# Four raw weight buffers in attention, PSUM pools kept open for six blocks of M, and another set-up ahead of the first scores

## The chip, the cores and the metric

One core of one Trainium2 chip. The metric is the device time of one execution in microseconds. Three runs of the kernel before are shown, and one execution with the hardware profiler, from which all rows below come.

## The reference

Causal attention with a bias from cumulative sums, then two layers on its 2304 x 512 output, all in float32; the weights come as float64 numbers.

```python
cum  = cumsum(max(s, 0), axis=-1)                      # q, k, v: 4 batches, 8 heads, 576 x 64
scores = where(causal, -1e9, q @ k.T / 8 + min(-(cum_i - cum_j), 0))
attn = softmax(scores) @ v                             # x: 2304 x 512
y = ((x @ w1) * (x @ w2) @ w3) @ w_out                 # w1, w2: 512 x 1024, w3: 1024 x 1024, w_out: 1024 x 512
h = y @ w_in                                           # 512 x 1024
solu = h * softmax(h)
out = layernorm(solu) * g_ln @ w_out2                  # 1024 x 512
```

## The kernel before, in words

Every product of the layers is made from float32 numbers split in a high and a low f32r word, three matmuls for each (high x high, high x low, low x high). The work is staged as follows.

**Attention** runs over 32 heads in the steps loop (L555). Per head: the scores (`sc`, L170 and L178/L179), row maxima on DVE (L192, into `STAT`), the exponential on ACT (L196), sums and reciprocals (`normalise`, L225 to L233), transposes on PE (`tr`, L265 to L281) and the product with V (`av`, L298). POOL makes the low words of the scores' operands (L100, `QK`).

**The first layer** runs under attention in `ab_unit` (L326): a = x w1, copied to SBUF by ACT (`a_sb`, L338), b = x w2, and DVE's product g = a b out of PSUM (`g_sb`, L346), which goes to DRAM. The last batch's units have no attention beside them; they fill PE from about 325 to 393 us.

**Weights** come as raw pairs of 32-bit words, 512 KB to a load (L407, the `stage` tiles), and are made into float32 by one ACT instruction (L363) and three of DVE (L369, L370, L374), then into a high word (ACT, L95) and a low word (DVE, L100). A list of jobs sets their order. `load_jobs` issues loads as long as fewer than `stg[1]` are out, and `pump(n)` converts n of them; the table PUMP says how many are converted in which step. In attention `stg` is two buffers of the pool `at`; for M it is set to four buffers of another pool.

**M** = w3 w_out is one matrix for two layers. `m_unit(f)` (L632 to L642) makes one of its eight blocks: 24 matmuls of 128x512 (L637) into one PSUM tile, then `MH` on ACT and `ML` on DVE (L100). The words of w3 are two tiles `w3h` and `w3l` per block half, converted in M's stage, with other weights (`IT..`, `IB..`) among them. The loop over f stands at L909 and following.

**The second layer and the rest**: x = g M in `x2_half` (L721; `gh` and `gl` are the words of g, read back from DRAM), then h (L753), the softmax and layer norm, turned tiles (L817) and the output (L847).

PSUM tiles come from two pools at a time, `PSP`. During attention's last part they are `psE` (two banks) and `psF` (six). These are closed at L662, ahead of M, and `psC` and `psD` (four each) are opened in their place.

The order of instructions on each engine is not the program's own: a scheduler with a simulated timeline sets it, and `tc.issue_after` pins an instruction behind another. So an edit in one place can move instructions in others.

**The start** (L481 to L533): eight dummy products of zeros (`zp`, L485) on PE; s loaded into one half of `s_zero`, whose other half POOL sets to zero as the scan's second operand; POOL's memsets of the operands' extra rows (`aug_rows`: two blocks of zeros, a pair of rows of ones and one of -1 for each of two heads); on DVE the scaling (L504) and the scan (L505); then the loads of the sums (`load_aug`, L148 and L149), DVE's memsets for the third head (L512 to L514), POOL's diagonal mask (L521, L522) and its constants for `STAT`, `PT` and `VT` (L527 to L532).

Of the kernel before, what the change touches and what calls it, by code (L numbers as in the profile page):

```python
# [8 lines left out]
F32 = mybir.dt.float32  # L9
# [3 lines left out]
AF = mybir.ActivationFunctionType  # L13
ALU = mybir.AluOpType
AX = mybir.AxisListType
PSUM = bass.MemoryType.PSUM
# [10 lines left out]
def tile_attention_moe(  # L27
# [15 lines left out]
    nc = tc.nc  # L43
    B, H, D, _, S = qkT.shape
    NH = B * H
# [6 lines left out]
    HS = S // 2  # L52
# [4 lines left out]
    for i in range(4, 0, -1):  # L57
# [7 lines left out]
    ps_ctx = ExitStack()  # L65
    PSP = [
        ps_ctx.enter_context(tc.tile_pool(name="psA", bufs=2, space=PSUM)),
        ps_ctx.enter_context(tc.tile_pool(name="psB", bufs=4, space=PSUM)),
    ]
# [38 lines left out]
    wmask = at.tile([128, S], F32, name="wmask")  # L108
# [284 lines left out]
    jobs = []  # L393
    loaded = []

    stg = [at, 2]

    def stage(src):
        raw = stg[0].tile([128, CW, 2], U32, tag="stage", bufs=stg[1], name="stage")
# [83 lines left out]
    zp = smalltile("zp")  # L483
    for i in range(8):
        nc.tensor.matmul(zp[:, 0:HS], zz[:, 0:128], zz, start=True, stop=True)  # L485
    s_zero = at.tile([NH, 2, S], F32, tag="qk2", bufs=2, name="s_zero")
    s_sb, zero = s_zero[:, 0], s_zero[:, 1]
    nc.sync.dma_start(out=s_sb, in_=s.rearrange("b h t -> (b h) t"))
    load_head(0)
    if NQ >= 1:  # L490
        load_head(1)
    cum = at.tile([NH, 2, S], F32, tag="qk2", bufs=2, name="cum")[:, 0]
    CK = at.tile([NH, 2, S], F32R, tag="P", bufs=PB, name="CK")
    nc.gpsimd.memset(zero, 0.0)

    def aug_rows(q_, k_):
        nc.gpsimd.memset(q_[0:64].bitcast(F32), 0.0)
        nc.gpsimd.memset(k_[0:64].bitcast(F32), 0.0)
        nc.gpsimd.memset(q_[0:2].bitcast(F32), 1.0)
        nc.gpsimd.memset(k_[32:34].bitcast(F32), -1.0)  # L500

    for i in range(2):
        aug_rows(QN[i], KN[i])
    nc.vector.tensor_scalar(out=s_sb, in0=s_sb, scalar1=0.0, scalar2=1.0 / SCALE, op0=ALU.max, op1=ALU.mult)  # L504
    nc.vector.tensor_tensor_scan(out=cum, data0=s_sb, data1=zero, initial=0.0, op0=ALU.add, op1=ALU.add)  # L505
    for i in range(2):
        load_aug(i, cum[i:i + 1])

# [1 line left out]
    QN.append(qk3[:, 0])  # L510
    KN.append(qk3[:, 1])
    nc.vector.memset(qk3[0:64], 0.0)  # L512
    nc.vector.memset(qk3[0:2, 0], 1.0)
    nc.vector.memset(qk3[32:34, 1], -1.0)  # L514
    load_head(2)
    load_aug(2, cum[2:3])
    nc.sync.dma_start(out=cumf_scr, in_=cum)
    hi(CK[:, 0], cum, nc.vector)
    lo(CK[:, 1], cum, CK[:, 0])
    nc.sync.dma_start(out=cum_scr.bitcast(F32), in_=CK.bitcast(F32))  # L520
    nc.gpsimd.memset(wmask, 0.0)  # L521
    nc.gpsimd.affine_select(  # L522
        out=wmask[:, S - 128:S], in_=wmask[:, S - 128:S], pattern=[[-1, 128]],
        compare_op=ALU.is_ge, fill=NEG / SCALE, base=0, channel_multiplier=1,
    )
    for st in STAT:
        nc.gpsimd.memset(st, 1.0)  # L527
    for t in PT:
# [1 line left out]
            nc.gpsimd.memset(t[64:128, KO[j]:KO[j] + 64], 0.0)  # L530
    for t in VT:
        nc.gpsimd.memset(t[64:128, 4], 0.0)  # L532
    nc.sync.dma_start(out=gln, in_=g_ln.rearrange("(k p) -> p k", p=128))  # L533

    for f in range(KF):
# [96 lines left out]
    def m_unit(f):  # L632
        ps = smalltile("m")
        for k in range(KF):
            H3, L3 = m_st[f, k // 4]
            for w_, o_ in ((H3, WOH), (H3, WOL), (L3, WOH)):
                nc.tensor.matmul(  # L637
                    ps, w_[:, k % 4], o_[:, k],
                    start=(k == 0 and w_ is H3 and o_ is WOH), stop=(k == KF - 1 and w_ is L3),
                )  # L640
        hi(MH[:, f], ps)
        lo(ML[:, f], ps, MH[:, f])  # L642
# [8 lines left out]
    for i in range(8):  # L651
# [7 lines left out]
            nm[0] += 1  # L659
    behind.clear()  # L660
    right0.close()
    ps_ctx.close()  # L662
    PSP[:] = [
        ctx.enter_context(tc.tile_pool(name="psC", bufs=1, space=PSUM)),
        ctx.enter_context(tc.tile_pool(name="psD", bufs=4, space=PSUM)),
    ]
    HD = DF // 2

    r2 = ctx.enter_context(tc.tile_pool(name="r2", bufs=1, side="right"))
# [239 lines left out]
        wf_load(i)  # L909
    load_g(1)  # L910
    for f in range(nm[0], KF):
        m_unit(f)
        pump(AM[f])
        if f < 6:
            wf_words(f)
        if f == 5:
            split_g(0)
# [101 lines left out]
```

## Time and profile before

| | us |
|---|---|
| median of 3 runs | 738.95 (737.88 to 739.62) |
| the profiled execution's own time | 737.73 |
| its span | 736.0 |
| mean granted clock of TensorE | 0.997 |
| PE busy in the span | 716.7 |
| DVE busy | 504.9 |
| ACT busy | 468.0 |
| POOL busy | 99.5 |

The times of the rows count from the span's start; the profiled execution's time is 1.7 us more than its span. A row of a timeline shows when an instruction began, how long it took, its engine, line and tiles, and in brackets how long the engine had been idle just before it and whose end let it go. PE's matmuls are pipelined, so one can begin before the one ahead of it has ended.

### The profile page before, as it was taken

Reading aid. Unit: us, or ns where it says so; the run is one execution under the profiler, and the core shown is the slowest. Engines: PE = TensorE matmul, PEld = TensorE weight load, DVE = VectorE, ACT = ScalarE, POOL = GpSimd, SP = SyncE. Lnnn points to the kernel's source line nnn. Section 1 sums busy time; section 2 is a strip of 40 time slices with the busy share of each in tenths; the row PEclk is TensorE's granted clock in tenths of the full one; section 3 lists DMA queues with packets and bytes.
Section 4 is the critical chain, followed back from the end, with each engine's and each line's share of the span. In section 5 each row is a group of like instructions: output and inputs, shape, how many; then the busy total and the mean of one; then the engine's idle time right before and its main releaser. Section 6 shows DMA issues by size and latency. Waiting matters only on the chain.

```text
span 736.0 us, 13040 instructions
## 1 busy us (share of the span) xinstructions
PE 716.7 (97%) x4682; PEld 625.0 (85%) x4682; DVE 504.9 (69%) x1267; ACT 468.0 (64%) x985; POOL 99.5 (14%) x102
## 2 busy tenths in 40 slices
PE   9889998999999999999998999999999999999997
PEld 6567978888888899899997889988888988888886
DVE  7987978897678888632887876576747365563651
ACT  4987777898766777732544745577646465564652
POOL 5033313142221331000000000001000000000000
PEclk9999999999999999999999999999999999999999
DMA  4644554655476665614566943253234142304221
GB/s 109 186 126 99 174 161 142 194 144 130 127 221 186 182 188 149 208 61 147 170 215 202 355 149 101 58 110 75 79 82 101 44 123 75 89 12 75 44 57 44
DMA packets 79829, 95.52 MB, mean 130 GB/s; under 512 B 41418, under 2 KB 52682, under 8 KB 79764
## 3 DMA queue, kind: packets, MB, share of 16 engines
q1 hardware_dynamic: 79764, 94.69, 45.0%
q8 instruction: 37, 0.61, 0.3%
q14 instruction: 28, 0.23, 0.1%
HBM read 59.04 MB, written 20.14 MB: 108 GB/s over the span
## 4 chain that ended last, share of the span: by engine, by line
PE 73%; DVE 11%; DMA 8%; ACT 5%; issue 2%; POOL 1%; SPq 0%; ACTq 0%; DVEq 0%; POOLq 0%
PE x L721 14%; PE o L847 13%; PE b L326 10%; PE a L326 10%; PE hX L753 5%; DMA stage<-in_w_dram 5%; PE av L298 4%; PE hZ L753 3%; PE tr L265 3%; ACT P L196 2%; PE sc L170 2%; PE sc L178 2%; DVE P L192 2%; DVE stage L374 2%; PE hW L753 2%
## 5 line engine op out<-in xcount | busy, mean ns | idle before, releaser
L196 ACT ACTIVATE P<-P,STAT 128x576 f32<-128x576 f32 (+4 forms) x160 | 88.3, 554 | 31.5 <-DVE STAT L192 30.9
L100 POOL TENSOR_TENSOR QK<-qk,QK 64x1152 fp32r<-64x1152 f32 x24 | 67.1, 2798 | 167.2 <-ACT QK L95 158.9
L721 PE MATMUL x<-gl,MH 128*128 128x256 f32 x288 | 80.4, 280 | 0.0
L721 PE MATMUL x<-gh,ML 128*128 128x256 f32 x288 | 80.2, 279 | 0.0
L721 PE MATMUL x<-gh,MH 128*128 128x256 f32 x288 | 79.9, 280 | 0.0
L192 DVE CUSTOM_DVE_ANT_0 P<-sc,wmask 128x576 f32<-128x576 f32 (+4 forms) x160 | 70.6, 478 | 4.5 <-PE sc L170 3.2
L326 PE MATMUL a<-xT0h,W 128*128 128x288 f32 x256 | 58.1, 300 | 1.9 <-ACT a_sb L338 1.9
L326 PE MATMUL b<-xT0h,W 128*128 128x288 f32 x256 | 57.6, 299 | 1.5 <-DVE STAT L192 0.8
L847 PE MATMUL o<-OH,lh 128*128 128x512 f32 x144 | 57.1, 397 | 0.2 <-DVE ll L100 0.2
L326 PE MATMUL a<-xT1h,W 128*128 128x288 f32 x256 | 57.2, 298 | 0.0
L847 PE MATMUL o<-OH,ll 128*128 128x512 f32 x144 | 57.0, 396 | 0.0
L847 PE MATMUL o<-OL,lh 128*128 128x512 f32 x144 | 57.0, 396 | 0.0
L326 PE MATMUL b<-xT1h,W 128*128 128x288 f32 x256 | 56.5, 295 | 0.0
L721 PEld LDWEIGHTS x<-gl,MH 128*128 128x128 f32 x288 | 54.2, 188 | 1.3
L817 DVE COPY lt<-turned 128x2048 uint16<-128x2048 uint16 x16 | 21.9, 1368 | 48.4 <-DMA turned<-half 48.4
L721 PEld LDWEIGHTS x<-gh,MH 128*128 128x128 f32 x288 | 54.0, 188 | 1.1
L721 PEld LDWEIGHTS x<-gh,ML 128*128 128x128 f32 x288 | 54.1, 188 | 0.9
L346 DVE TENSOR_TENSOR g_sb<-b,a_sb 128x288 f32<-128x288 f32 x64 | 28.8, 449 | 32.8 <-PE b L326 16.7
L363 ACT ACTIVATE stage<-stage 128x512 f32<-128x512 f32 x56 | 36.9, 674 | 21.2 <-DMA stage<-in_w_dram 18.0
L298 PE MATMUL av<-PT,VT 128*64 128x64 f32 (+4 forms) x384 | 50.1, 395 | 0.0
L231 ACT ACTIVATE P<-P,STAT 128x576 f32<-128x576 f32 x64 | 42.7, 717 | 10.4 <-DVE STAT L226 10.4
L338 ACT ACTIVATE a_sb<-a 128x288 f32<-128x288 f32 x64 | 25.6, 401 | 33.3 <-PE a L326 33.1
(193 smaller groups left out, 1965.5 us busy)
## 6 DMA issues: line engine op xcount, KB each, us to landing
stage<-in_w_dram SPq DMA_DIRECT2D x32, 512.0 KB
g_scr<-g_sb SPq DMA_DIRECT2D x32, 288.0 KB
stage<-in_wo_dram SPq DMA_DIRECT2D x16, 512.0 KB
qk<-in_qk_dram SPq DMA_DIRECT2D x24, 288.0 KB
QK<-QK SPq DMA_DIRECT2D x24, 288.0 KB
gl<-g_scr SPq DMA_DIRECT2D x24, 256.0 KB
wf<-wf_scr SPq DMA_DIRECT2D x22, 256.0 KB
out_dram<-o SPq DMA_DIRECT2D x18, 256.0 KB
```

The lines of the kernel that those rows point to most:

```text
L100: eng.tensor_tensor(out=dst, in0=src, in1=hi_.bitcast(F32), op=ALU.subtract)
L192: mx = nc.vector.tensor_tensor_reduce(out=dst2, in0=ps_in, in1=msk, scale=-SCALE, scalar=BIG, op0=ALU.add, op1=ALU.min, accum_out=st[0:row ...
L196: ex = nc.scalar.activation(out=dst, in_=dst, func=AF.Exp, bias=st[0:rows, ti:ti + 1], scale=-1.0, accum_out=st[0:rows, 5 + ti:6 + ti],)
L231: nc.scalar.activation(out=dst, in_=dst, func=AF.Copy, scale=r)
L298: nc.tensor.matmul(st["ps"][64 * e:64 * e + 64, 448 + c0:448 + c1], vr[:, j, e], PT[(2 * p + e) % 4][:, o + c0:o + c1], **kw,)
L326: nc.tensor.matmul(ps, w_[:, c, fs], x_[:, c, sl], start=(c == 0 and w_ is WH and x_ is XH), stop=(c == KC - 1 and w_ is WL),)
L338: ab_last[0] = nc.scalar.activation(out=a_sb, in_=ps, func=AF.Copy).ins
L346: ab_last[1] = nc.vector.tensor_tensor(out=g[:, sl], in0=ps, in1=st["a"], op=ALU.mult).ins
L363: nc.scalar.activation(out=high.bitcast(F32), in_=high.bitcast(F32), func=AF.Copy, scale=2.0 ** -112)
L721: last = nc.tensor.matmul(ps[:, a], w_[:, k, m * 128:m * 128 + 128], g_[:, k % 2], start=(k == 0 and w_ is MH and g_ is GH), stop=(k == KF ...
L753: last_h[0] = nc.tensor.matmul(ps, x_[:, k], w_[:, k], start=first and k == 0 and x_ is XH and w_ is WH, stop=k == 1 and x_ is XL, skip_gr ...
L847: nc.tensor.matmul(ps, l_[:, k], w_[:, k], start=(k == 0 and l_ is LH and w_ is OH), stop=(k == KF - 1 and l_ is LL),)
```

## The change

In attention the staged weight loads get four raw buffers where there were two. The closing of `psE` and `psF` moves from ahead of M into the loop over M's blocks, ahead of block 6, so that blocks 0 to 5 use tiles of the old pools. At the start, the scan's second operand is the mask tile, which POOL has set to zero; POOL zeroes the first head's operands and DVE the second's; the rows of ones and of -1 are made by six ACT instructions out of `zz`; and POOL's constants for `STAT`, `PT` and `VT` are pinned behind the diagonal mask, which has to wait for the scan.

```diff
-    stg = [at, 2]
+    stg = [at, 4]
...
-    s_zero = at.tile([NH, 2, S], F32, tag="qk2", bufs=2, name="s_zero")
-    s_sb, zero = s_zero[:, 0], s_zero[:, 1]
+    s_sb = at.tile([NH, 2, S], F32, tag="qk2", bufs=2, name="s_sb")[:, 0]
...
-    nc.gpsimd.memset(zero, 0.0)
+    nc.gpsimd.memset(wmask, 0.0)
...
+    def const_rows(q_, k_):
+        for dst, src, value in ((q_[0:2], zz[0:2], 1.0), (k_[32:34], zz[32:34], -1.0)):
+            nc.scalar.activation(
+                out=dst.rearrange("p (a s) -> p a s", a=2), in_=src[:, None, :].broadcast_to((2, 2, HS)),
+                func=AF.Copy, scale=0.0, bias=value,
+            )
+
-    for i in range(2):
-        aug_rows(QN[i], KN[i])
+    for i, eng in enumerate((nc.gpsimd, nc.vector)):
+        eng.memset(QN[i][0:64], 0.0)
+        eng.memset(KN[i][0:64], 0.0)
+        const_rows(QN[i], KN[i])
-    nc.vector.tensor_tensor_scan(out=cum, data0=s_sb, data1=zero, initial=0.0, op0=ALU.add, op1=ALU.add)
+    nc.vector.tensor_tensor_scan(out=cum, data0=s_sb, data1=wmask[0:NH], initial=0.0, op0=ALU.add, op1=ALU.add)
...
-    nc.vector.memset(qk3[0:2, 0], 1.0)
-    nc.vector.memset(qk3[32:34, 1], -1.0)
+    const_rows(QN[2], KN[2])
...
-    nc.gpsimd.memset(wmask, 0.0)
-    nc.gpsimd.affine_select(
+    diagonal = nc.gpsimd.affine_select(
...
+    behind_scan = tc.issue_after(diagonal.ins)
+    behind_scan.__enter__()
     for st in STAT:
         nc.gpsimd.memset(st, 1.0)
...
+    behind_scan.__exit__(None, None, None)
...
-    ps_ctx.close()
-    PSP[:] = [
-        ctx.enter_context(tc.tile_pool(name="psC", bufs=1, space=PSUM)),
-        ctx.enter_context(tc.tile_pool(name="psD", bufs=4, space=PSUM)),
-    ]
...
     for f in range(nm[0], KF):
+        if f == 6:
+            ps_ctx.close()
+            PSP[:] = [
+                ctx.enter_context(tc.tile_pool(name="psC", bufs=1, space=PSUM)),
+                ctx.enter_context(tc.tile_pool(name="psD", bufs=4, space=PSUM)),
+            ]
         m_unit(f)
```

What this does to the order of the instructions is shown at three places. The words in brackets are the semaphores that an instruction waits on, by the engine or the DMA queue that raises them.

PE at the seventh block of M (block 6). Before, blocks run into each other; the rows here are the end of block 6, its first word pair's successor, and the second-layer matmuls that the scheduler put among blocks 6 and 7:

```order
L637 MATMUL m<-WOL,w3h 128x512
L637 MATMUL m<-WOH,w3l 128x512
L637 MATMUL m<-WOH,w3h 128x512 [waits Activation_49]
L637 MATMUL m<-WOL,w3h 128x512
L637 MATMUL m<-WOH,w3h 128x512 [waits Activation_49]
L637 MATMUL m<-WOL,w3h 128x512
L721 MATMUL x_5286<-gh_5214,MH 128x256 [waits DMAHW4_49,DMAHW3_49,DMAHW5_49,DMAHW2_49,DMAHW6_49,DMAHW1_49,DMAHW7_49,DMAHW0_49,DVE_49]
L721 MATMUL x_5286<-gl_4910,MH 128x256
```

And with the change, from the end of block 5 to the beginning of block 6:

```order
L646 MATMUL m<-WOH,w3h 128x512
L646 MATMUL m<-WOL,w3h 128x512
L646 MATMUL m<-WOH,w3l 128x512
L646 MATMUL m<-WOH,w3h 128x512 [waits DVE_49]
L646 MATMUL m<-WOL,w3h 128x512
```

The first matmul of block 6 now has a wait on DVE; before, 20 matmuls of the second layer stood in one row behind L721's first, now three stand there.

DVE at the same place with the change (`ML` is the low word of a block of M, `IT..` low words of other weights, L369 to L374 conversions):

```order
L374 SCALAR_TENSOR_TENSOR stage<-stage 128x512 [waits DVE_49]
L100 TENSOR_TENSOR IT3l<-wf,IT3h 128x512 [waits DMAHW7_49,Activation_49]
L370 SCALAR_TENSOR_TENSOR stage<-stage 128x512 [waits DVE_49]
L100 TENSOR_TENSOR ML<-m,MH 128x512 [waits Activation_49]
L100 TENSOR_TENSOR w3l<-stage,w3h 128x512 [waits PE_49,Activation_49] x2
L374 SCALAR_TENSOR_TENSOR stage<-stage 128x512 [waits DVE_49]
```

This `ML` is block 5's. The order of the kernel before has it at the same place, behind the same conversions but one.

DVE in attention, between the maxima of two heads (`P,STAT_117` and `P,STAT_116`), before:

```order
L192 ISA P,STAT_117<-sc,wmask 128x576 [waits PE_49]
L192 ISA STAT_117 128x1
L374 SCALAR_TENSOR_TENSOR stage<-stage 128x512 [waits DVE_49]
L192 ISA P,STAT_116<-sc,wmask 128x448 [waits PE_49]
L192 ISA STAT_116 128x1
```

With the change:

```order
L192 ISA P,STAT_117<-sc,wmask 128x576 [waits PE_49]
L192 ISA STAT_117 128x1
L369 TENSOR_SCALAR stage<-stage 128x512 [waits DMAHW5_49]
L369 TENSOR_SCALAR stage<-stage 128x512 [waits DMAHW6_49]
L374 SCALAR_TENSOR_TENSOR stage<-stage 128x512 [waits DVE_49]
L100 TENSOR_TENSOR W_124<-stage,W_123 128x4x128 [waits Activation_49]
L192 ISA P,STAT_116<-sc,wmask 128x448 [waits DVE_49,PE_49]
L192 ISA STAT_116 128x1
```

Three instructions of conversion more stand ahead of the second head's 128x448 maxima.

## Rows read from the trace of the kernel before

**Rows 1.** The page's first part: busy time, share of the span, instructions.

```profile
PE 716.7 (97%) x4682; PEld 625.0 (85%) x4682; DVE 504.9 (69%) x1267; ACT 468.0 (64%) x985; POOL 99.5 (14%) x102
```

**Rows 2.** Windows: length; busy PE, PEld, DVE, ACT, POOL (instructions); clock, DMA share, GB/s.

```profile
78.00:104.00 26.00, 23.69 (x178) 21.93 (x177) 25.35 (x76) 22.95 (x63) 8.88 (x3) 1.00 0.51 142
...
104.00:160.00 56.00, 53.03 (x409) 46.35 (x408) 47.27 (x136) 44.87 (x110) 14.40 (x5) 1.00 0.56 168
...
22.00:23.00 1.00, 0.56 (x3) 0.19 (x2) 1.00 (x4) 1.00 (x4) 0.00 (x0) 1.00 1.04 321
```

**Rows 3.** Timeline of PE in attention: start, length, instruction, idle before and its releaser.

```profile
102.11 0.40 PE L326 MATMUL b<-xT0h,W 128*128 128x288 f32 x1 [0.56 <-DVE STAT L192]
...
123.76 0.37 PE L178 MATMUL sc<-QK 128*128 128x288 f32 x1 [1.60 <-issue]
...
158.74 0.40 PE L326 MATMUL b<-xT0h,W 128*128 128x288 f32 x1 [0.28 <-DVE STAT L192]
...
310.96 0.40 PE L326 MATMUL a<-xT0h,W 128*128 128x288 f32 x1 [1.20 <-ACT a_sb L338]
```

**Rows 4.** DVE's waits in 60 to 160 and in 280 to 320: total, times, longest.

```profile
DVE stage L369 <- DMA stage<-in_w_dram: 10.0, 8, 3.1
...
DVE stage L369 <- DMA stage<-in_wo_dram: 5.7, 3, 2.8
```

**Rows 5.** Timeline of ACT around 310 us.

```profile
309.93 0.68 ACT L363 ACTIVATE stage<-stage 128x512 f32<-128x512 f32 x1 [1.33 <-DMA stage<-in_wo_dram]
```

**Rows 6.** Timeline of all engines at the start.

```profile
1.24 7.19 PE L485 MATMUL zp<-zz 128*128 128x288 f32 x16 [1.24 <-DVE zz L482]
...
2.66 2.00 DVE L504 TENSOR_SCALAR s_zero<-s_zero 32x576 f32<-32x576 f32 x1 [1.47 <-DMA s_zero<-in_s_dram]
...
8.66 6.32 PE L170 MATMUL sc<-QKN 128*128 128x288 f32 x24 [0.23 <-DMA QKN<-cum]
```

**Rows 7.** Timeline of PE from the last first-layer matmuls to block 6 of M.

```profile
393.24 0.29 PE L326 MATMUL b<-xT1l,W 128*128 128x288 f32 x1
393.38 0.29 PE L326 MATMUL b<-xT1h,W 128*128 128x288 f32 x1
395.72 0.50 PE L637 MATMUL m<-WOH,w3h 128*128 128x512 f32 x1 [2.05 <-DVE g_sb L346]
...
398.19 0.63 PE L637 MATMUL m<-WOL,w3h 128*128 128x512 f32 x1
398.62 0.63 PE L637 MATMUL m<-WOH,w3l 128*128 128x512 f32 x1
...
430.11 0.39 PE L637 MATMUL m<-WOH,w3h 128*128 128x512 f32 x1
```

**Rows 8.** The chain that ended last, at the end of M: start, length, piece.

```profile
439.20 5.00 PE m L637 x22
444.20 8.99 PE x L721 x77
```

**Rows 9.** Windows, one us of M behind the wait (columns as in rows 2).

```profile
397.00:398.00 1.00, 1.00 (x4) 0.81 (x3) 0.77 (x2) 0.71 (x1) 0.00 (x0) 0.50 0.47 180
```

**Rows 10.** Timeline of DVE in M.

```profile
415.32 0.43 DVE L369 TENSOR_SCALAR stage<-stage 128x512 uint32<-128x512 uint32 x1 [2.20 <-DMA stage<-in_w_dram]
...
433.43 0.69 DVE L100 TENSOR_TENSOR ML<-m,MH 128x512 fp32r<-128x512 f32 x1
```

**Rows 11.** Timeline of DVE: low words of staged weights in attention.

```profile
84.02 1.96 DVE L100 TENSOR_TENSOR W<-stage,W 128x512 fp32r<-128x512 f32 x1
...
86.59 2.46 DVE L100 TENSOR_TENSOR W<-stage,W 128x512 fp32r<-128x512 f32 x1
...
99.59 1.79 DVE L100 TENSOR_TENSOR W<-stage,W 128x512 fp32r<-128x512 f32 x1
...
102.97 0.65 DVE L100 TENSOR_TENSOR W<-stage,W 128x512 fp32r<-128x512 f32 x1
```

**Rows 12.** Timeline of POOL in the same stretch.

```profile
82.74 5.76 POOL L100 TENSOR_TENSOR QK<-qk,QK 64x1152 fp32r<-64x1152 f32 x2 [13.42 <-ACT QK L95]
```

## The prediction, before the changed kernel was run

> **What bounds the kernel now.** I read the page's busy shares first: PE is busy for 716.7 of 736.0 us, DVE for 504.9, ACT for 468.0 [rows 1]. So there are only some 19 us that any edit of waits can win, and the next question is where they lie. The timeline of PE answers it, by the idle that it prints behind an instruction: apart from the start and the tail there are idle spots up to 160 us, one at 311 us and one ahead of M at 395.72 us [rows 3, 7]. The table by windows gives their sums: PE is busy for 23.69 of the 26.00 us from 78 to 104, so 2.31 are idle, and for 53.03 of the 56.00 from 104 to 160, so 2.97 [rows 2]. Elsewhere between 160 and 393 us, and from 444 us on, PE has no idle that matters: a delay or a gain in M reaches the end one for one, because everything behind it is PE's own work (the chain of waits is a chain of PE rows there [rows 8]).
>
> The two groups of idle spots are not alike. In 78 to 104 us DVE itself is busy for 25.35 of 26.00 [rows 2]: PE waits there for an engine without slack, as in the spot at 102.11 us, which ends with the row statistics of L192 [rows 3]. In 104 to 160 us, and ahead of 311 us, the wait on a staged load comes first: the table of DVE's waits puts 10.0 us in 8 waits on the load that L369 reads, up to 3.1 us each, in the stretch 60 to 160, and 5.7 us in 3 waits in 280 to 320 [rows 4]. On ACT the same shows as 1.33 us ahead of the L363 at 309.93, which takes 0.68 [rows 5]; the `a_sb` copy of L338 is queued behind it, and PE's 1.20 us at 310.96 end with that copy [rows 3].
>
> **The change part by part.**
>
> *Four raw buffers.* Loads go out one or two places earlier on SP, four together at the first. A conversion that waits for its load no longer holds DVE and ACT. I count as gone the four spots between 123.76 and 158.74 us (all 2.97 us of that window) and the 1.20 at 310.96 [rows 2, 3]. A spot costs a little more than its idle: matmuls follow each other at 393.38 - 393.24 = 0.14 us (0.13 over several), while one alone takes 0.29 [rows 7], so each restart loses another 0.16. Sum: 2.97 + 1.20 + 5 x 0.16 = 4.97 us won. Lower bound: only the two that are longest go, 1.60 + 1.20 + 2 x 0.16 = 3.1. I take the upper end, since DVE's 10.0 us of waiting is over three times the idle that it gave to PE.
>
> On SP two loads of attention rows (L161) now stand behind a staged load. A staged load is 512 KB, at 321 GB/s [rows 2] 1.63 us. I take nothing for it, since no spot of [rows 3] ends with a load of attention rows; with that cover gone it is 2 x 1.63 = 3.3 us.
>
> The 2.31 us in 78 to 104 I leave as they are: no load ends them. There the same edit moves work the wrong way: the order shows three conversions more (two L369, one low word of L100) ahead of the 128x448 maxima of one head, and six to eight by the next head. Bounds are zero and 2.31 + 4 x 0.16 = 2.95 gained, and 3.4 lost (first rival); zero is nearest to what the rows show, since the number of conversions is the same and only their place changes.
>
> *The start.* ACT's rows of ones and the shorter POOL queue can bring the first scores forward only to where the eight dummy products end: those occupy PE from 1.24 for 7.19, so to 8.43, and the first score matmul is at 8.66 with 0.23 idle [rows 6]. So 0.23 is the ceiling, and I take it. DVE's two new memsets lie in its 1.47 us of idle ahead of L504 [rows 6], and DVE loses two memsets later. POOL's held constants come after the scan, ahead of the time of first use. If that cover were gone, the loss would be that of seven memsets of some 0.5 us.
>
> *PSUM pools.* This part has two effects of opposite sign. First, M's first product no longer waits for the last `g_sb` on DVE; it waits for ACT alone, which is done. PE's 2.05 us ahead of 395.72 go, and M starts at 393.38 + 0.13 = 393.51 [rows 7]. With them goes the clock: after that idle the granted clock is 0.50 from 397 to 398 us, the level of 1.2 GHz [rows 9], matmuls follow at 398.62 - 398.19 = 0.43 us instead of 5.00 / 22 = 0.227 [rows 7, 8], and over eight of them that is 8 x 0.20 = 1.6 us.
>
> Second, the wait comes back ahead of block 6. Its first matmul opens the new pools, and by the order it waits for DVE: for the last eviction out of the old pools, the `ML` of block 5. That `ML` stands on DVE behind a queue with no idle. Before, DVE comes out of a wait for a load at 415.32, then works without a break; its `ML` of block 5 is at 433.43, 18.1 us and 32 instructions later [rows 10]. The order leaves all but one of them (31), and the load that opens the run is one of M's, whose buffers are not part of the change. So that `ML` starts at 433.43 - 0.57 = 432.86 and ends with its 0.69 at 433.55. PE is there long before: 144 matmuls of six blocks at 0.227 from 393.51 end at 426.2. **PE idles for 7.3 us**, then starts block 6 at 433.57, where before it began it at 430.11 [rows 7]. The 21 second-layer matmuls that filled PE among blocks 6 and 7 before are not there to help; three are left, by the order.
>
> From there: 48 matmuls x 0.227 = 10.91, three of L725 at 8.99 / 77 = 0.117 = 0.35 [rows 8], and the clock lost again after the idle: nothing at best, 1.6 as behind the 2.05 us of idle above, or 2.9 as in the cold start, where 16 passes took 7.19 / 16 = 0.449 and the 24 behind them 6.32 / 24 = 0.263 (16 x 0.186 = 2.9) [rows 6]. The idle is longer than the one that cost 1.6 and the array is not as cold as at the start, so 2.2. M ends at 433.57 + 10.91 + 0.35 + 2.2 = 447.03. To stand where before stood at 444.20 - 0.17 = 444.03 (all of M and 21 of L721 done [rows 8]) 18 more second-layer matmuls are needed: 18 x 0.117 = 2.10, so 449.13. **M costs 5.1 us**, between 2.9 and 5.8 by the clock's bounds.
>
> **Sum**: -0.23 - 4.97 + 5.1 = -0.1 us. The profiled execution took 737.73, 1.2 below the median of the three runs shown, 738.95; the sum taken from either leaves it where it was. I predict 738.9 against the median. With the bounds of the gaps and of the clock the forecast's own range is 736.5 to 741.5. A measurement of this kernel can tell about 0.2%, 1.5 us, from no change.
>
> **The rivals.**
>
> *Conversions in the way (slower).* In 78 to 104 us DVE has 0.65 us to spare [rows 2]. Six conversions more ahead of the maxima, at the 18.1 / 32 = 0.57 us at which DVE takes one in M [rows 10], are 3.4 us, all of it on the path of the softmax that PE waits for: 738.9 + 3.4 = 742.3. It decides once more than the 1.5 us that a run can tell, two or three conversions, reach PE. There is a second way to nearly the same price. A low word `W` takes 0.65 us alone, at 102.97, but 2.46 at 86.59 [rows 11], while POOL's L100 has 5.76 us of work from 82.74 on [rows 12]: 1.81 us more. Three such words are held so before the change, from 84.02 to 99.59 [rows 11], and two more would give 3.6. The Trainium skill's page "SBUF — State Buffer", section "Who interferes with whom", states a rule for this: a DVE instruction with two inputs in SBUF and a GpSimd instruction that reads SBUF exclude each other, and the one that comes second waits for the whole of the other. The trace agrees, with the 0.65 and the 2.46. For it: no slack there, and the order shows the words moved. Against it: a conversion that is done early is missing later, and one of the words may now come ahead of POOL's start at 82.74.
>
> *The DVE-bound spots go too (faster).* Once loads are never awaited, the same work starts earlier, and DVE may enter 78 us with less left to do. All of 2.31 + 4 x 0.16 = 2.95 us goes: 736.0. Against it: those spots wait for DVE, which stays busy.
>
> *Block 6 does not wait.* If the new pools take over bank by bank, or `ML` of block 5 is done early, the change does more than I read in it: M is then bound by its `w3` words on DVE, whose last come where they came before, so M costs about nothing and 738.9 - 5.1 = 733.8 is left. Against it: one wait on DVE stands in the order at that matmul, and DVE's queue ahead of it is full.
>
> **How the numbers follow.** Forecast 0.50, of which 0.34 within 0.2%, 0.09 faster (the clock costs nothing after the idle) and 0.07 slower (it costs as in the cold start and the small spots stay). Conversions in the way 0.25, slower. DVE-bound spots gone 0.20, faster. Block 6 without wait 0.05, faster. So faster 0.34, same 0.34, slower 0.32. The range from 735.4 to 742.6 takes in the first rival's price and the second's, and leaves out the last and the ends where two mishaps add up.
>
> **What would show it.** Right: the table of DVE's waits without L369's 10.0 and 5.7 us; no PE idle at 124 and 311 us; first scores at about 8.4 us; M's first product without a wait; then some 7 us of idle ahead of the first L646 of block 6, ended by DVE, and a granted clock near 0.5 for some us behind it. Wrong: block 6 starting within 2 us of the end of block 5, a longer sum of PE idle in 78 to 104 us, or low words of over 1.5 us in larger number than three.

## The result, and the profile after

The changed kernel takes 746.39 us (median of 6 runs, 744.73 to 748.31) against 738.82 before: a ratio of 1.0107 [1.0089, 1.0126], 7.6 us slower. The forecast was 738.9. The profiled execution took 744.73 with a span of 742.9 and a mean granted clock of 0.991; the other five had 0.984 to 0.986.

The page's busy shares, to hold against [rows 1]:

```profile
PE 718.5 (97%) x4682; PEld 627.4 (84%) x4682; DVE 506.8 (68%) x1267; ACT 471.5 (63%) x991; POOL 94.2 (13%) x95
```

PE is busy for nearly as long; the span has 6.9 us more, 5.1 of them idle on PE. The clock is a part of both: span times what the mean granted clock lacks to 1 is 736.0 x 0.003 = 2.2 us before and 742.9 x 0.009 = 6.7 us after. This is an estimate of what the clock took, and an upper one: in M of the changed kernel the clock lacks 3.41 us from 390 to 460 us, a part of it while PE idles, and costs 2.4 (worked out below). Four points that both traces have show where they came in: the first score matmul, the last matmul of the first layer, the start of M's last matmul with 21 matmuls of the second layer behind PE (the changed kernel has done 3 of them by its last `m`, at 448.55, so 18 x 0.117 are added), and the last matmul. The third is called the end of M from here on.

| | before | after | difference |
|---|---|---|---|
| first scores | 8.66 | 7.78 | -0.88 |
| last first-layer matmul | 393.38 | 396.55 | +3.17 |
| end of M | 443.81 | 450.66 | +6.85 |
| last matmul | 731.85 | 738.81 | +6.96 |

So in these two executions attention lost 4.05 us behind the start's 0.88, M 3.68, and the rest 0.11.

**Attention.** DVE's waits in 60 to 160 us, the longest first, to hold against [rows 4]:

```profile
DVE PT L97 <- PE tr L265: 3.8, 1, 3.8
DVE stage L370 <- ACT stage L363: 2.8, 2, 1.9
DVE STAT L225 <- ACT P L196: 2.5, 2, 1.7
```

The 10.0 us on staged loads are gone from the top of the table, as are the 5.7 us around 300 us. But PE's idle spots (stretches in which PE has no matmul) have not gone. They are fewer and longer; the timeline of PE, to hold against [rows 3]:

```profile
79.44 0.47 PE L178 MATMUL sc<-QK 128*128 128x448 f32 x1 [0.93 <-DVE g_sb L346]
...
91.90 0.61 PE L326 MATMUL b<-xT0h,W 128*128 128x288 f32 x1 [2.67 <-DVE g_sb L346]
...
106.37 0.40 PE L326 MATMUL b<-xT0h,W 128*128 128x288 f32 x1 [2.15 <-DVE STAT L192]
...
131.26 0.37 PE L326 MATMUL b<-xT0h,W 128*128 128x288 f32 x1 [2.81 <-DVE g_sb L346]
```

All end with DVE. From 60 to 165 us the trace of before has 8 spots with 5.19 us in sum, none over 1.7; this one has 4 with 8.56. And behind two of them the clock is at its lower level; windows (columns as in rows 2):

```profile
78.00:104.00 26.00, 22.40 (x156) 20.58 (x155) 25.01 (x65) 21.08 (x50) 8.39 (x3) 0.93 0.53 154
104.00:160.00 56.00, 50.97 (x384) 44.63 (x383) 45.98 (x131) 42.84 (x108) 13.67 (x5) 0.97 0.53 153
...
93.00:94.00 1.00, 1.00 (x6) 1.00 (x6) 1.00 (x7) 0.78 (x3) 0.00 (x0) 0.50 0.92 288
```

Summed over windows of one us from 60 to 165, what the granted clock lacks to 1 is 3.42 us, where before it was 0.00. The spot at 311 us is gone, worth 1.20. Together: -0.88 for the start, +3.37 of idle, +3.42 of clock, -1.20, and -0.80 for five restarts less at 0.16 is +3.9; 3.17 were measured, and 0.7 stay unexplained. The 0.00 of before is one execution's; the table behind experiment 15 has others with the same order of instructions that lost as much clock as the changed kernel.

What DVE does in front of the spots, in its timeline:

```profile
83.92 2.70 DVE L370 SCALAR_TENSOR_TENSOR stage<-stage 128x512 uint32<-128x512 uint32 x1
...
87.23 2.44 DVE L370 SCALAR_TENSOR_TENSOR stage<-stage 128x512 uint32<-128x512 uint32 x1
...
101.48 2.55 DVE L374 SCALAR_TENSOR_TENSOR stage<-stage 128x512 uint32<-128x512 uint32 x1
...
125.30 3.17 DVE L374 SCALAR_TENSOR_TENSOR stage<-stage 128x512 uint32<-128x512 uint32 x1
```

and POOL at the same times:

```profile
83.40 5.72 POOL L100 TENSOR_TENSOR QK<-qk,QK 64x1152 fp32r<-64x1152 f32 x2 [15.09 <-ACT QK L95]
100.82 2.67 POOL L100 TENSOR_TENSOR QK<-qk,QK 64x1152 fp32r<-64x1152 f32 x1 [11.70 <-ACT QK L95]
...
124.97 2.95 POOL L100 TENSOR_TENSOR QK<-qk,QK 64x1152 fp32r<-64x1152 f32 x1 [2.92 <-ACT QK L95]
```

A conversion that takes 0.68 us elsewhere takes 2.4 to 3.2 where it meets POOL's subtraction (called held below): four of them. Before, three low words were held [rows 11, 12], and two conversions more that neither these rows nor the prediction name:

```profile
132.38 2.03 DVE L369 TENSOR_SCALAR stage<-stage 128x512 uint32<-128x512 uint32 x1 [1.64 <-DMA stage<-in_w_dram]
...
148.37 1.85 DVE L374 SCALAR_TENSOR_TENSOR stage<-stage 128x512 uint32<-128x512 uint32 x1
```

What conversions and low words with two inputs took over 0.68 us each sums from 60 to 165 us to 5.5 us before and 8.3 us after. So the hold grew by under 3 us.

**M.** The timeline of PE, to hold against [rows 7]:

```profile
396.55 0.29 PE L326 MATMUL b<-xT1h,W 128*128 128x288 f32 x1
396.68 0.39 PE L646 MATMUL m<-WOH,w3h 128*128 128x512 f32 x1
...
435.11 0.79 PE L646 MATMUL m<-WOH,w3h 128*128 128x512 f32 x1 [5.62 <-DVE ML L100]
435.70 0.63 PE L646 MATMUL m<-WOL,w3h 128*128 128x512 f32 x1
436.12 0.63 PE L646 MATMUL m<-WOH,w3l 128*128 128x512 f32 x1
436.55 0.63 PE L646 MATMUL m<-WOH,w3h 128*128 128x512 f32 x1
```

M begins without a wait, 0.13 us behind the first layer. Ahead of block 6 PE idles for 5.62 us until block 5's `ML` is out, then runs at 0.43 us a matmul. DVE at that place (against [rows 10]), and the clock there:

```profile
416.86 0.43 DVE L369 TENSOR_SCALAR stage<-stage 128x512 uint32<-128x512 uint32 x1 [0.49 <-DMA stage<-in_w_dram]
...
434.37 0.68 DVE L100 TENSOR_TENSOR ML<-m,MH 128x512 fp32r<-128x512 f32 x1
```

```profile
437.00:438.00 1.00, 1.00 (x4) 0.81 (x3) 0.40 (x1) 0.56 (x1) 0.00 (x0) 0.50 0.00 0
```

### The profile page after: what moved, and what is told of

It reads as the page before. It is cut to its first block, busy times and chain, and to the rows that moved or that the text cites. A ratio compares the mean times of both kernels' runs of the same rounds, so it can differ in the third digit from the quotient of the medians.

```text
span 742.9 us, 13034 instructions
## 1 busy us (share of the span) xinstructions
PE 718.5 (97%) x4682; PEld 627.4 (84%) x4682; DVE 506.8 (68%) x1267; ACT 471.5 (63%) x991; POOL 94.2 (13%) x95
## 4 chain that ended last, share of the span: by engine, by line
PE 82%; DVE 9%; DMA 3%; ACT 3%; issue 3%; SPq 0%; DVEq 0%; ACTq 0%
PE x L725 14%; PE o L851 13%; PE b L326 12%; PE a L326 12%; PE av L298 6%; PE hX L757 5%; PE tr L265 4%; PE hZ L757 3%; PE sc L178 2%; DMA stage<-in_w_dram 2%; PE sc L170 2%; PE sc L179 2%; PE m L646 2%; DVE stage L374 2%; DVE stage L370 2%
## 5 line engine op out<-in xcount | busy, mean ns | idle before, releaser
L100 POOL TENSOR_TENSOR QK<-qk,QK 64x1152 fp32r<-64x1152 f32 x24 | 65.6, 2736 | 174.2 <-ACT QK L95 174.0
L326 PEld LDWEIGHTS b<-xT0h,W 128*128 128x128 f32 x256 | 43.9, 192 | 8.7 <-ACT PT L95 3.0
```

The lines of the kernel that those rows point to most:

```text
L100: eng.tensor_tensor(out=dst, in0=src, in1=hi_.bitcast(F32), op=ALU.subtract)
L326: nc.tensor.matmul(ps, w_[:, c, fs], x_[:, c, sl], start=(c == 0 and w_ is WH and x_ is XH), stop=(c == KC - 1 and w_ is WL),)
```

## The experiments

All ratios are to runs of the kernel before on the same chip. The diffs are against the changed kernel unless another is named. A ratio has an interval of about 0.002 either way, so a difference of two has about 0.003, or 2 us. The state of the theory when the first four were written: each part acts by itself, and what attention lost is POOL's hold on DVE's conversions.

**1. Two raw buffers again.**

```diff
-    stg = [at, 4]
+    stg = [at, 2]
```

> The changed kernel with two raw buffers again: new start and late closing of the PSUM pools stay. Theory (each part acts by itself; the four buffers cost about 4.8 us in attention, the pools 3.7, the start gives 0.9): 738.8 + 3.7 - 0.9 = 741.6 us, PE's idle spots in attention as in the kernel before, none with 2.67 or 2.81 us, DVE's wait on staged loads back. Rival (the pools cost all of it and the buffers give what was forecast): about 750 us. Rival (attention lost by the new start, not by the buffers): stays at about 746 us.

743.71 us, 1.0059 [1.0035, 1.0083], 4.6 us over its own before (739.11), where the theory had 2.8. The three long spots are gone, the small ones of before are back. The four buffers cost 1.0107 - 1.0059 = 0.0048, 3.5 us, less than the 4.8 of the theory. Ahead of block 6 the idle is longer still, as PE comes to M earlier:

```profile
434.45 0.80 PE L646 MATMUL m<-WOH,w3h 128*128 128x512 f32 x1 [6.52 <-DVE ML L100]
```

**2. Pools closed ahead of M again.**

```diff
     right0.close()
+    ps_ctx.close()
+    PSP[:] = [
+        ctx.enter_context(tc.tile_pool(name="psC", bufs=1, space=PSUM)),
+        ctx.enter_context(tc.tile_pool(name="psD", bufs=4, space=PSUM)),
+    ]
...
-        if f == 6:
-            ps_ctx.close()
...
```

> The changed kernel with the old PSUM pools closed ahead of M, as before the change: new start and four buffers stay. Theory: 746.4 - 3.7 = 742.7 us; first-layer units end at about 396.5 us as in the changed kernel, M's first product waits some 2 us for the last product on DVE, block 6 has no wait for an eviction. Rival (what M lost is only what attention handed on): about 746 us.

741.23 us, 1.0018 [1.0001, 1.0035]. The spots of 2.20, 2.17 and 2.83 us are there, M waits 2.45 us for DVE and block 6 not at all. The late closing costs 1.0107 - 1.0018 = 0.0089 here, 6.6 us, where the theory had 3.7.

**3. The start alone.** Experiment 2's edit and this one:

```diff
-    stg = [at, 4]
+    stg = [at, 2]
```

> The new start alone on the kernel before: two buffers, pools closed ahead of M. Theory: first scores at about 7.8 us instead of 8.66 and nothing else moved on PE, so 738.8 - 0.9 = 737.9 us. Rival (the gain is lost again in attention, where PE waits for DVE anyway): 738.8 us. My forecast on record had 0.23 us for it: 738.6.

738.91 us, 0.9991 [0.9968, 1.0014]: a gain of 0.7 that these runs can't tell from none. The scores began at 8.16 us in this trace; the same code began them between 7.1 and 8.25 in the other kernels, since the dummies' passes come up to speed at different times. Against this kernel the first one prices the pools at 0.0068, 5.0 us, and the second the buffers at 0.0027, 2.0 us, which by itself is not clear of nothing.

**4. POOL writes, but does not read.** The low words of q and k are left out: POOL fills their place with zeros.

```diff
-        lo(t[64:128, 1::2], raw, t[64:128, 0::2], G)
+        G.memset(t[64:128, 1::2].bitcast(F32), 0.0)
```

> The changed kernel, where POOL fills the low words of the scores' operands with zeros by a memset instead of making them by a subtraction that reads SBUF: the low words of q and k are left out. DVE's order is the same. Theory (DVE's two-input conversions are held while POOL's reading instruction runs, and that makes the idle spots and takes the clock): no conversion on DVE over 0.8 us in 60 to 160 us, the spots of 2.67 and 2.81 us gone or under 1 us, the granted clock 1.00 there, time 738 to 741 us. Rival (the conversions are simply too many ahead of the maxima): conversions at 0.68 us, but spots of over 2 us stay, time at 744 us or more.

740.82 us, 1.0010 [0.9985, 1.0034]. No two-input conversion in 70 to 165 us takes over 0.69 us; the longest spot is 1.31 us and the clock is 1.00 from 78 to 160. So the hold of two-input conversions is real and it goes when POOL doesn't read. A shift of L369, which has one input, still took 1.08 us at 115.91 instead of 0.42, beside a memset. The memset is also shorter (1.06 us) than the subtraction, which the next run takes out.

**5. POOL writes for as long.** Three of those memsets, 3 x 1.10 = 3.3 us.

```diff
-        lo(t[64:128, 1::2], raw, t[64:128, 0::2], G)
+        for _ in range(3):
+            G.memset(t[64:128, 1::2].bitcast(F32), 0.0)
```

> The changed kernel, where POOL writes zeros three times over the low words of the scores' operands, so that it is busy about as long as with its subtraction (some 2.7 us) but reads nothing: the low words of q and k are left out. DVE's order is that of the changed kernel. Theory (DVE is held by POOL's reading, not by the lateness of POOL's result): conversions at 0.7 us, no idle spot of over 2 us in 78 to 160 us, first-layer units end at about 390 to 391 us as with the single memset, time 740 to 741 us. Rival (POOL's short memset freed the scores earlier, and that was the gain): spots of over 2 us come back and the time is at 745 us or more.

742.08 us, 1.0048 [1.0031, 1.0064]. From 70 to 165 us two-input conversions take 0.69 us or less but for one of 0.97; the shifts with one input (L370 in this kernel) take up to 1.38 beside the memsets. One spot of 2.33 us is back at 100.40, ended by DVE's maxima. The time lies between theory and rival. So the hold costs, and something else that POOL's longer work brings; the lateness of what it makes and the longer shifts aren't told apart.

**6. The same edit on the kernel before.**

> The kernel before with the same three memsets on POOL in place of its subtraction (the low words of q and k are left out). Theory: the three low words that POOL holds before the change are at 0.7 us too, some 4.3 us of DVE won in 84 to 101 us, and PE's spots there shrink by up to 2.3 us: 736 to 737 us. With the run beside it, four buffers then cost nothing or give up to 3 us once POOL does not hold DVE. Rival (POOL's hold never mattered before the change, since the spots there end with other work): 738.5 to 739.5 us.

739.09 us, 1.0010 [0.9994, 1.0026]: the rival. With POOL's memsets the two kernels differ by 0.0038; take off the pools' 0.0068 and put the start's 0.0009 back, and the four buffers are at -0.0021. The intervals of the four ratios in this sum come to some 0.005 either way, so it shows neither a gain nor a loss.

**7. The idle ahead of block 6 filled.** To the kernel of experiment 1:

```diff
+        if f == 5:
+            extra = smalltile("fill")
+            H3, L3 = m_st[f, 1]
+            for k in range(28):
+                nc.tensor.matmul(extra, H3[:, k % 4], WOH[:, 4 + k % 4], start=True, stop=True)
```

> The new start and the late closing of the pools with two raw buffers, as in the first run of the study, and behind block 5 of M 28 more matmuls of 128x512 into a PSUM tile that nobody reads: 28 x 0.227 = 6.4 us, as long as PE's idle there. Theory (the granted clock falls behind that idle, and costs about 2.3 us): no matmul of block 6 at a spacing of 0.43 us, time 743.7 - 2.3 = 741.4 us. Rival (the clock is not what costs, or the work ahead of block 6 only delays it): 743.7 us or more.

744.45 us, 1.0067 [1.0043, 1.0091]: not faster. In the trace no matmul behind block 5 runs at 0.43, and from the last first-layer matmul to the end of M it takes 52.6 us instead of 55.2. Of these 2.6 us 1.7 are lost again behind M (289.8 us from its end to the last matmul instead of 288.2), as in experiment 14. And attention ended at 397.52 in this execution, 2.5 us later than in experiment 1's, with the same instructions on PE in the same order.

**8. Pools closed behind M.** Experiment 1's kernel, with the close ahead of the second layer's first product.

```diff
-        if f == 6:
-            ps_ctx.close()
...
+    ps_ctx.close()
+    PSP[:] = [
+        ctx.enter_context(tc.tile_pool(name="psC", bufs=1, space=PSUM)),
+        ctx.enter_context(tc.tile_pool(name="psD", bufs=4, space=PSUM)),
+    ]
     mctx.close()
```

> The new start, two raw buffers, and the old PSUM pools kept for all eight blocks of M, closed ahead of the second layer's first product. Theory: M's first product without a wait, no wait for an eviction between blocks; PE waits in small pieces for the words of blocks 6 and 7, then some 2 us for the last eviction ahead of the second layer; 738.8 - 0.7 - 1.5 = 736.6 us, if the pieces stay short enough for the clock. Rival (PE waits in one piece of over 2 us, and the clock falls again): 739 to 741 us.

741.18 us, 1.0036 [1.0018, 1.0055]: the rival, at its upper end. PE waits in one piece for the words of block 6, then for the last eviction:

```profile
431.18 0.50 PE L646 MATMUL m<-WOH,w3h 128*128 128x512 f32 x1 [2.21 <-ACT w3h L95]
433.59 0.80 PE L646 MATMUL m<-WOH,w3l 128*128 128x512 f32 x1 [0.47 <-DVE w3l L100]
...
444.84 0.39 PE L725 MATMUL x<-gh,MH 128*128 128x256 f32 x1 [1.41 <-DVE ML L100]
```

Its granted clock is 0.94 in the mean of 400 to 460 us. Without second-layer work to fill in, an earlier M only waits elsewhere.

**9 and 10. POOL's subtraction in four pieces**, with four buffers (experiment 2's kernel) and with two (experiment 3's).

```diff
-        lo(t[64:128, 1::2], raw, t[64:128, 0::2], G)
+        for a in range(2):
+            for c in range(0, S, S // 2):
+                cs = slice(c, c + S // 2)
+                lo(t[64:128, 1 + 2 * a, cs], raw[:, a, cs], t[64:128, 2 * a, cs], G)
```

> The new start, four raw buffers, pools closed ahead of M (the second run of the study, 1.0018 of before), and POOL's subtraction for the low words of the scores' operands cut into four of 64x288. Theory (DVE's two-input instructions wait for the whole of the POOL instruction that came first, so a shorter one holds them for less): no conversion on DVE over 1.6 us in 78 to 160 us, the spots of 2.20 and 2.83 us shorter than 1.5 us, 2 to 4 us won: ratio to before 0.996 to 0.999. Rival (DVE and POOL now take turns, and POOL's result is late by as much): spots of over 2 us ended by POOL's low words, ratio 1.002 or more.

> The same four pieces on POOL, with two raw buffers: the new start alone and pools closed ahead of M (the third run of the study, 0.9991 of before). Theory: the three low words held for 1.8 to 2.5 us take under 1.4 us, 1 to 2 us won: ratio 0.996 to 0.998. Rival (as with POOL writing only, where the kernel before gained nothing): ratio 0.998 to 1.001.

736.1 us, 0.9963 [0.9936, 0.9990], the theory, and 738.08 us, 1.0003 [0.9982, 1.0024], the rival. With four buffers a spot of 2.09 us stays where less than 1.5 was expected. The longest conversion or low word there is 1.30 us, as expected:

```profile
86.09 1.30 DVE L100 TENSOR_TENSOR W<-stage,W 128x512 fp32r<-128x512 f32 x1
```

Here four buffers are better than two by 0.0040, 3.0 us, the only pair of kernels in which POOL reads and they are. The hold doesn't explain it: conversions and low words took 6.5 us over 0.68 each from 60 to 165 us with four buffers, and 1.5 with two.

**11 and 12. DVE makes those low words** for heads 10 to 17, with four buffers (experiment 2's kernel) and with two (experiment 3's).

```diff
-        lo(t[64:128, 1::2], raw, t[64:128, 0::2], G)
+        lo(t[64:128, 1::2], raw, t[64:128, 0::2], V if 10 <= h < 18 else G)
```

> The new start, four raw buffers, pools closed ahead of M, and the low words of the scores' operands of heads 10 to 17 made by DVE instead of POOL. Theory: no POOL work holds DVE in 78 to 160 us; each takes DVE some 1.3 us (64x1152), about as long as it was held for each before, but the scores' operands come 1.4 us earlier: ratio 0.997 to 1.001. Rival (DVE has no room in 78 to 104 us): spots of over 2 us there, ratio 1.002 or more.

> The same low words on DVE, with two raw buffers: the new start alone and pools closed ahead of M. Theory: as in the run beside it, with DVE's waits on staged loads taking up the work: ratio 0.996 to 0.999. Rival (DVE has no room in 78 to 104 us): ratio 1.001 or more.

736.66 us, 0.9966 [0.9946, 0.9985], and **734.27 us, 0.9931 [0.9906, 0.9957]**: the second beats the kernel before and the changed one. Both are better than the theory's range. Each low word takes DVE 1.35 us, less than a held conversion loses. The windows of the second have no lack of clock from 78 to 160 and 3.12 us of idle:

```profile
78.00:104.00 26.00, 24.01 (x175) 21.81 (x174) 23.66 (x71) 21.71 (x55) 0.00 (x0) 1.00 0.48 131
104.00:160.00 56.00, 54.87 (x422) 47.95 (x421) 51.62 (x151) 48.63 (x121) 2.65 (x1) 1.00 0.62 179
```

But the buffers still cost 0.0035, 2.6 us, with no POOL work from 78 to 140 us. That speaks against the theory that the hold is all of it, and experiment 15 has the same again.

**13 and 14. The late closing on the fastest kernel**, plain and with experiment 7's matmuls; the first is experiment 1's kernel, the second experiment 7's, each with this edit:

```diff
-        lo(t[64:128, 1::2], raw, t[64:128, 0::2], G)
+        lo(t[64:128, 1::2], raw, t[64:128, 0::2], V if 10 <= h < 18 else G)
```

> The fastest kernel so far (new start, two raw buffers, low words of heads 10 to 17 on DVE, 0.9931 of before), with the old PSUM pools closed ahead of block 6 as in the change. Theory: the late closing costs 5 us by itself wherever attention ends: 5.5 to 7 us of idle ahead of block 6, matmuls at 0.43 us behind it; ratio 0.998 to 1.002. Rival (the cost came from attention's lateness, which made the eviction late): ratio 0.993 to 0.996.

> The kernel of the run beside it, with 28 matmuls of 128x512 behind block 5 that nobody reads, in the idle ahead of block 6. Theory (of the 5 us, 2 to 2.6 are the granted clock behind the idle): matmuls of block 6 at 0.23 us at once, ratio lower than in the run beside it by 0.003 (2 to 2.6 us). Rival (the clock costs nothing here): the same ratio within 0.001, or higher.

740.13 us, 0.9988 [0.9969, 1.0008], the theory, and 739.63 us, 0.9994 [0.9979, 1.0008], the rival. The late closing costs 0.9988 - 0.9931 = 0.0057, 4.2 us, by itself, with 6.03 us of idle. Filling it wins nothing, though block 6 runs at full speed: from its first matmul to the end of M the trace takes 13.2 us instead of 14.9. It is given back in the second layer, where the filled kernel has two spots that the plain one lacks:

```profile
429.23 0.47 PE L646 MATMUL m<-WOH,w3h 128*128 128x512 f32 x1 [1.03 <-DVE ML L100]
...
517.44 0.50 PE L762 MATMUL hX<-IT2h,XWh 128*128 128x512 f32 x1 [0.80 <-ACT so L768]
...
522.92 0.50 PE L762 MATMUL hX<-IT3h,XWh 128*128 128x512 f32 x1 [0.59 <-ACT so L768]
```

0.80 + 0.59 and two restarts at 0.16 are 1.7 us, the whole win. What made ACT late there wasn't tried.

**15. The whole change, DVE making those low words** (the same edit on the changed kernel).

> The whole change (four raw buffers, late closing of the pools, new start) with the low words of the scores' operands of heads 10 to 17 made by DVE instead of POOL. Theory (attention's loss was POOL's hold on DVE; what is left is the pools' 5 us): between 0.998 and 1.003 of before, where the change itself was at 1.0107. Rival (the hold was a part of the loss only, the rest is the early conversions): 1.005 or more.

742.25 us, 1.0025 [1.0011, 1.0038]: 0.0082 better than the changed kernel, 6.1 us, and in the theory's range. Against experiment 13, its twin with two buffers, the four buffers cost 0.0037, 2.7 us. Its trace has a spot ended by DVE, and the lower clock behind it.

```profile
98.50 1.95 PE L265 MATMUL tr<-ident,P 128*128 128x128 f32 x10 [2.02 <-DVE P L233]
...
78.00:104.00 26.00, 22.23 (x149) 19.96 (x148) 25.78 (x75) 22.53 (x55) 0.00 (x0) 0.90 0.55 164
```

From 84 to 97 us DVE does eleven instructions of conversion here, at most 0.69 us each; its twin does seven from 82 to 96.

The idle spots and the lack of clock from 60 to 165 us side by side, one profiled execution each; the last column is the time from the first score matmul to the last first-layer matmul:

| kernel | buffers | spots | idle, us | longest, us | clock lost, us | attention, us |
|---|---|---|---|---|---|---|
| before | 2 | 8 | 5.19 | 1.60 | 0.00 | 384.7 |
| exp. 1 | 2 | 9 | 5.92 | 1.60 | 1.71 | 387.4 |
| exp. 3 | 2 | 8 | 7.09 | 1.62 | 3.42 | 390.6 |
| exp. 7 | 2 | 8 | 6.44 | 1.60 | 3.42 | 389.3 |
| exp. 8 | 2 | 6 | 4.52 | 1.60 | 3.41 | 386.2 |
| changed | 4 | 4 | 8.56 | 2.81 | 3.42 | 388.8 |
| exp. 2 | 4 | 5 | 8.55 | 2.83 | 3.40 | 388.9 |
| exp. 4, one memset | 4 | 7 | 5.42 | 1.31 | 0.00 | 382.5 |
| exp. 5, three memsets | 4 | 6 | 5.52 | 2.33 | 1.70 | 384.6 |
| exp. 6, three memsets | 2 | 4 | 4.21 | 1.66 | 3.42 | 386.7 |
| exp. 9, pieces | 4 | 4 | 4.94 | 2.09 | 1.70 | 384.7 |
| exp. 10, pieces | 2 | 7 | 6.52 | 1.69 | 0.00 | 386.3 |
| exp. 11, DVE's words | 4 | 5 | 5.31 | 2.02 | 3.42 | 387.2 |
| exp. 15, DVE's words | 4 | 4 | 5.31 | 2.02 | 3.42 | 385.3 |
| exp. 12, DVE's words | 2 | 6 | 2.82 | 0.92 | 0.00 | 385.1 |
| exp. 13, DVE's words | 2 | 8 | 2.15 | 0.45 | 0.00 | 382.5 |
| exp. 14, DVE's words | 2 | 4 | 1.23 | 0.45 | 0.00 | 381.8 |

The first five kernels have the same instructions on PE, DVE and ACT in the same order from the first scores to M, and so have the next two. Yet the clock took anything from 0.00 to 3.42 us from the five, and no spot of theirs is over 1.7 us; experiment 3's trace shows the lower level behind spots of 1.62, 0.75 and 1.60 us:

```profile
127.40 0.58 PE L178 MATMUL sc<-QK 128*128 128x288 f32 x1 [1.60 <-issue]
...
129.00:130.00 1.00, 1.00 (x5) 1.00 (x6) 1.00 (x4) 1.00 (x4) 1.00 (x1) 0.50 0.98 198
```

The execution of before is the fastest of the five: their mean is 387.6 us, and the two with four buffers are 1.2 us above that, not 4.05. What four buffers cost is therefore read from timed runs. Span times what the mean granted clock lacks to 1, in the mean of all timed runs of a kernel, estimates the time that the clock took (from above, as said; the clock is given to 0.001, which is 0.7 us of a span):

| pair, four and two buffers | ratio, difference | clock's time, us | difference, us |
|---|---|---|---|
| changed, exp. 1 | 0.0048 (3.5 us) | 10.3, 8.0 | 2.3 |
| exp. 2, exp. 3 | 0.0027 (2.0 us) | 6.5, 5.0 | 1.5 |
| exp. 11, exp. 12 | 0.0035 (2.6 us) | 4.7, 1.7 | 3.0 |
| exp. 15, exp. 13 | 0.0037 (2.7 us) | 8.1, 5.8 | 2.3 |
| exp. 9, exp. 10 | -0.0040 (-3.0 us) | 4.5, 4.1 | 0.3 |

In the four pairs in which four buffers lose, most of the loss is clock by this estimate. At which spots the timed runs lost it they do not show.

## Why the prediction was wrong

**The start** was mis-sized: -0.23 forecast, -0.88 in the trace, -0.7 in timed runs within their interval. The dummies' end at 8.43 was taken as fixed; here their 16 passes took 6.71 us instead of 7.19, and the scores follow them. The change leaves these passes as they were. With the new start they ended between 6.8 and 8.4 us, with the old one at 8.4 in both traces, and no run tells why; so how much of the 0.88 the change made is open.

**Four raw buffers** is the step that failed: "I count as gone the four spots between 123.76 and 158.74 us (all 2.97 us of that window) and the 1.20 at 310.96", 4.97 us won. The waits on loads did go, and so did the spot at 311. But the sum took the idle of 104 to 160 us as the price of the load, and kept 78 to 104 as it was. In the rows none of the four spots ends with a load: two of them are in [rows 3], ended by "issue" and by DVE's maxima, and the other two are

```profile
125.20 0.40 PE L326 MATMUL a<-xT0h,W 128*128 128x288 f32 x1 [0.67 <-ACT a_sb L338]
...
134.83 0.41 PE L274 MATMUL tr<-ident,P 64*64 64x64 f32 x4 [0.42 <-DVE g_sb L346]
```

The runs price the buffers at a loss of 2.0 to 3.5 us instead. With two buffers a late load kept conversions back, and DVE took the maxima and the products in the meantime; with four, the conversions are ready, the order has them ahead, and PE waits for DVE in long pieces.

**The first rival comes nearest**, in both of its ways. Conversions stand in front of what PE waits for (experiment 15, no POOL near), and a conversion that meets POOL's subtraction takes 2.4 to 3.2 us (experiments 4 and 5 took the reading away and the long ones went). But it was priced in idle alone, at 742.3 to 742.6. In M I had priced the clock, in attention I put it at nothing without a reason: behind two of the three spots of over 2 us it lacks 3.4 us in the profiled execution, and by the estimate from timed runs the clock is 1.5 to 3.0 us of what four buffers cost. That the long spots are what brings the clock down more often is argued, not shown: kernels with spots of 1.7 us at most lost 3.4 us in single executions too.

How the two ways share is not settled. With the subtraction moved to DVE the whole change gains 6.1 us, but the kernel with two buffers gains 0.0060, 4.4, as well: most of the hold was there before, 5.5 of 8.3 us by the traces. Buffers cost where POOL's subtraction is whole or DVE makes the words itself, and give 3.0 us with POOL's subtraction in pieces (experiments 9 and 10), with an interval nearly as wide. No one account here covers all five pairs; why pieces turn the sign stays open.

**PSUM pools** went as forecast in mechanism and nearly in size. M's first product lost its wait; block 6 got one, for block 5's `ML`. Forecast +5.1, in the profile +3.68, in timed pairs +5.0 and +4.2 (and +6.6 on four buffers). The idle was 5.62 instead of 7.3: the `ML` came out 435.05 - 396.55 = 38.5 us behind the last first-layer matmul instead of 40.2, since DVE waited 0.49 for the load that opens its run instead of 2.20. The clock was right: 448.55 + 0.23 less the start of block 6, 435.11, and 10.91 + 0.35 of work leaves 2.4 us; forecast 2.2, a choice between bounds of 1.6 and 2.9.

**Sum.** Without the buffers' step the forecast's own terms give 738.9 + 4.97 = 743.9, 4.9 us over before; experiment 1, which is that kernel, has 743.71, 4.6 us over its own before, with an interval of 2.6 to 6.1. The rest to 746.39 is what the buffers lost. The range ended at 742.6 because the rival's price was added to a forecast that still had the buffers' 4.97 us in it. As written the rival left that gain alone; the runs don't show it, and without it the rival's time is 743.9 + 3.4 = 747.3. That this is near 746.39 is in part luck, since its 3.4 us are idle and most of the loss is clock by the estimate above.

## What to carry to other kernels

A wait on a load that holds a shared engine also keeps that engine free for more urgent work: before counting such a wait as won, look at what will run in its place, and who waits behind it. Price an idle spot on TensorE with what the clock does behind it, and take that price from more than one execution: here five executions of one order differ by 3.4 us of clock and 5.9 us of time in attention. And a new PSUM pool in the place of old ones made PE wait for the last eviction out of them, 5.2 to 6.5 us in the kernels that close ahead of block 6 without filling in, so close pools where that engine's queue is short. When a rival puts its loss where the sum counts a gain, ask whether the gain survives, and if not take it out of the rival's time too.

## What the hardware showed that was not expected

The same idle spot takes the clock in one execution and not in another. At 51 to 53 us PE idles for 1.6 to 2.3 us in every kernel here; the four matmuls behind it took 1.13 us in the changed kernel and 2.08 in experiment 3:

```profile
51.53 1.13 PE L170 MATMUL sc<-QKN 128*128 128x320 f32 x4 [1.98 <-DVE STAT L192]
```

```profile
51.92 2.08 PE L170 MATMUL sc<-QKN 128*128 128x320 f32 x4 [1.98 <-DVE STAT L192]
```

This fits the spread of the timed runs: the kernel before lies between 736.3 and 746.4 us in the runs beside the last batches, at mean clocks of 0.985 to 0.999, the slower runs mostly at the lower clocks, while experiment 12 lies between 732.2 and 735.6 at 0.995 to 1.000. One profiled execution can be one that lost none in attention, as that of before did.

The Trainium skill's page "SBUF — State Buffer", section "Who interferes with whom", says that only a GpSimd instruction that reads SBUF shuts out a DVE instruction with two inputs there. The runs agree: 2.4 to 3.2 us in the changed kernel against POOL's subtraction; against its memsets 0.69 or less in experiment 4, and the same in experiment 5 but for one of 0.97, in the same order of instructions. The one-input shifts (L369) are another matter: one took 2.03 us against the subtraction before the change, and some took 1.08 to 1.38 against memsets, where they take 0.42 alone.
